# A spectral filter held in two buffers: its loads and stores cut in half by groups, and the second half moved behind the forward row moves

## The chip, the cores and the metric

The program runs on one core of one Trainium2 chip. The metric is the device time of one execution in microseconds (us), lower is better. Three runs of the kernel before took 339.59, 340.53 and 343.56 us, median 340.53. Five engines work side by side, each in its own program order: TensorE (PE, matmuls), VectorE (DVE), ScalarE (ACT), GpSimd (POOL) and SyncE (SP, which here does nothing but issue DMAs). An instruction of one engine waits for another's through semaphores.

## The reference

Forward, on x of 2048 x 448 in bf16, and then all gradients for a given output gradient:

```python
y  = irfft2(rfft2(layernorm(x)) * (w_r + 1j*w_i))      # over both axes; w_r, w_i: 2048 x 225
h  = x + y
u  = gelu(einsum("sd,sf->df", layernorm(layernorm(h)), w1) + b1)   # w1: 2048 x 1792
h2 = h + (einsum("df,fs->ds", u, w2) + b2).T                       # w2: 1792 x 2048
# results: h2 and the gradients of x, w_r, w_i, w1, b1, w2, b2
```

`w_r` and `w_i` are the filter. It is used twice: the forward transform is multiplied by it, and in the backward pass the gradient is multiplied by its conjugate, while the filter's own gradient (results `out_2` and `out_3`, of the same 2048 x 225 shape) is formed.

## The kernel before, in words

The order of PE, DVE, ACT and SP is that of the program text ("manual schedule"); only POOL's order is set by a planner. `clock`, `defer` and `fill` in the text serve that order: `fill(n)` puts n matmuls of an independent product between dependent ones, `defer` puts a DMA issue some matmuls later.

The stages around the change, in order:

- **Row stage** (loop over t in 0..15, lines 932 to 979). Tiles of x are normalised and folded on DVE, with the inverse standard deviations from Newton steps on POOL (`newton_gp`, lines 407 to 416). `row_a` and `row_b` (lines 661 and 671) turn them by two matmuls each. After every second `row_b` a **row move** (line 697) carries the result from SBUF to SBUF into `D2`; there are eight, seven issued by SP and the last by ACT. Between these stand matmuls of `dg` (line 845): 14 blocks of 16 matmuls of 128 x 448, which need block j of the transposed `w2`. Blocks 0 to 4 are turned on PE; **blocks 5 to 13 come by a DMA transpose each** (line 312), issued by SP into five slots. `cap` holds back blocks 9 to 13 until after the row loop (`held_w2`, lines 989 to 991).
- **Forward s2 stage** (`s2_stage`, line 704, called at line 999). Four sets s of four groups of 128 x 2 x 226. For each set PE does 48 small matmuls on `D2`, ACT copies the result to `Xs`, DVE multiplies by the filter (`w_mult`, line 753), and one turn later PE does 48 more on the product; the copies go by the **D3 moves** (line 740), four a set, into `D3`. The moves of the first three sets are issued by POOL, those of the last by SP, POOL and ACT. After that PE reads `D3` (`inv_rows`, line 765).
- **Backward**: the same s2 stage again (called at line 1384) with `bwd_mult` (line 1299), which also overwrites the filter by its gradient, set by set; then `inv_rows` with `gx_consumer` (line 1391), whose step t issues `GW_AT.count(t)` stores of that gradient. Between the small matmuls stand the weight gradients (`gw_gen`, line 1313), with their transposed inputs (`st_load`, `load_du`) and their stores, all on SP.

The filter lies in one buffer `rW` as (part c: real, imaginary) x (16 groups) x (225 columns) on 128 partitions; sets 0 and 1 use groups 0 to 7, sets 2 and 3 groups 8 to 15. Even partitions hold rows upward, odd partitions rows downward. `w_io` (line 580) is a generator of 18 DMAs, nine a part: four of 16 even partitions with 16 contiguous rows each (one run of 7200 bytes a partition), four of 16 odd partitions with rows in falling order (runs of 450 bytes), and one of 16 single rows. `W_AT` (line 924) says how many of the 18 loads are issued in which step t of the row loop; 14 go to SP, four to POOL (each behind a small clear on DVE, line 596, that keeps the planner from putting it earlier). All are issued by t = 6. The stores are the same 18 in the other direction, all on SP.

Of the kernel before, what the change touches and what calls it, by code (L numbers as in the profile page):

```python
# [124 lines left out]
def kernel(  # L125
# [123 lines left out]
    rW = region("rW", NG * 2 * KW)  # L249
# [326 lines left out]
    Wc = cut(rW, 0, 2, NG, DF)  # L576
    W = Wc.rearrange("p c g k -> p g c k")

    def w_io(dr, di, store):
        Wq = Wc.rearrange("(q s) c g k -> s q c g k", s=2)  # L580
        for c_, d in ((0, dr), (1, di)):
            moves = []
            for i in range(4):
                moves.append((Wq[0][16 * i:16 * i + 16, c_].rearrange("l g k -> l (g k)"), 16 * i, [[P * DF, 16], [1, 16 * DF]]))
                g0 = 0 if i else 1
                moves.append((Wq[1][16 * i:16 * i + 16, c_, g0:NG, :], P - 16 * i - g0,
                              [[P * DF, 16], [-DF, NG - g0], [1, DF]]))
            moves.append((Wq[1][0:16, c_, 0, :], 64, [[P * DF, 16], [1, DF]]))
            late = [m for n, m in enumerate(moves) if n in (0, 2, 4, 6)] if c_ and not store else []
            early = moves if not late else [m for n, m in enumerate(moves) if n not in (0, 2, 4, 6)]  # L590
            for n, (sb, row, dims) in enumerate(early + late):
                d_ap = bass.AP(d.tensor, d.offset + row * DF, dims)
                eng = nc.sync if n < len(early) else gp_
                if eng is gp_:
                    i = 32 * (n - len(early))
                    nc.vector.memset(Wc[i:i + 1, 1, 8, 0:1], 0.0)
                eng.dma_start(out=d_ap if store else sb, in_=sb if store else d_ap)
                yield
# [325 lines left out]
    W_AT = {**{t: 2 for t in range(6)}, 6: 6}  # L924
# [7 lines left out]
    for t in range(NT):  # L932
# [34 lines left out]
        if t in GROUPS:  # L967
            a, b = GROUPS[t]
            newton_gp(mvx[:, a:b, 1], rstd_x[:, a:b], slice(a, b))
        for _ in range(W_AT.get(t, 0)):  # L970
# [11 lines left out]
    for _ in w_loads:  # L982
        pass
# [4 lines left out]
    turn_biases, place_biases = load_biases()  # L988
    cap[0] = NFB
    while held_w2:  # L990
        held_w2.pop(0)()
    fill(4)
    gen_RT()
    fill(7)

    def fwd_mult(s, j, x, y):
        w_mult(x, set_of(W, s)[:, 2 * j:2 * j + 2], y, False)
# [485 lines left out]
```

## Time and profile before

| | |
|---|---|
| profiled execution, its own time | 340.34 us |
| its span, first to last instruction | 338.3 us |
| granted TensorE clock | 0.998 |
| PE busy | 330.2 us, 98% of the span |
| DVE, ACT, POOL busy | 251.7, 206.7, 84.6 us |
| DMA queue of SP and ACT's hardware path (q1) | 133288 packets, 73.13 MB, 84.5% of 16 engines' span |
| DMA queue of POOL (q0) | 2448 packets, 3.83 MB, 5.3% |
| runs | 339.59, 340.53, 343.56 us |

A busy PE is one on which some matmul is in flight, so 98% doesn't say that it is at its peak; the starts of its matmuls say where it stood. An SP row's time is the time of issuing, not of the transfer. "Idle before" stands in brackets behind the instruction that ended it, with what it waited for.

### The profile page before, as it was taken

How to read it: one execution, taken by the hardware profiler on the slowest of the kernel's cores; microseconds unless marked ns; L12 is line 12 of the kernel's file. 1: busy time of each engine (PE TensorE's matmuls, PEld its weight loads, DVE VectorE, ACT ScalarE, POOL GpSimd, SP SyncE). 2: the span in 40 equal slices, each digit the busy share in tenths (PEclk: the TensorE clock that was granted, in tenths of full speed). 3: DMA queues.
4: the chain of work that ended last, by engine and by line, in shares of the span. 5: the costliest groups of instructions: out<-in, count | busy, mean ns of one | idle time of the engine just before them, and what ended most of it. 6: DMA issues, size and time to landing. Idle time of an engine off the chain costs nothing.

```text
span 338.3 us, 7987 instructions
## 1 busy us (share of the span) xinstructions
PE 330.2 (98%) x2893; PEld 174.6 (52%) x2893; DVE 251.7 (74%) x670; ACT 206.7 (61%) x448; POOL 84.6 (25%) x254
## 2 busy tenths in 40 slices
PE   8999989999999999999999999999999999999995
PEld 4666554456545555555555555554344434555552
DVE  8998739827947888593227888786697993599994
ACT  6987666848965534423222346665588875588882
POOL 7767202412210000000001111210020222156670
PEclk9999999999999999999999999999999999999999
DMA  7999899959899999687877889837699999978885
GB/s 251 400 203 182 190 258 141 227 125 279 230 378 287 348 279 242 179 274 192 193 178 164 174 188 155 176 84 232 221 220 302 290 244 252 284 188 278 245 293 200
DMA packets 136198, 78.03 MB, mean 231 GB/s; under 512 B 86528, under 2 KB 127592, under 8 KB 136032
## 3 DMA queue, kind: packets, MB, share of 16 engines
q1 hardware_dynamic: 133288, 73.13, 84.5%
q0 software_dynamic: 2448, 3.83, 5.3%
q8 instruction: 22, 0.36, 0.5%
q10 hardware_dynamic: 424, 0.58, 0.5%
q14 instruction: 16, 0.13, 0.1%
HBM read 28.33 MB, written 22.04 MB: 149 GB/s over the span
## 4 chain that ended last, share of the span: by engine, by line
PE 83%; DVE 6%; DMA 4%; ACT 3%; issue 1%; POOL 1%; SPq 0%; DVEq 0%; ACTq 0%
PE ps_mm L220 68%; PE ps_ff L220 9%; PE ps_ff L225 3%; DMA r<-r 3%; ACT rO L84 2%; PE ps_mm L375 2%; DVE rS L84 2%; DVE r L84 1%; DMA r<-rX 1%; DVE rX L84 1%; DVE stats L84 1%; DVE rA L84 1%; ACT rE L84 1%; PE ps_mm L318 0%; DVE rG L84 0%
## 5 line engine op out<-in xcount | busy, mean ns | idle before, releaser
L220 PEld LDWEIGHTS <-r 128*128 128x128 bf16 (+2 forms) x628 | 58.6, 105 | 48.5 <-issue 3.0
L220 PEld LDWEIGHTS <-rS 128*128 128x128 bf16 (+1 forms) x468 | 36.2, 97 | 31.9 <-issue 6.0
L84 ACT CAST rO<-ps_mm 128x512 bf16<-128x512 f32 (+1 forms) x68 | 36.5, 584 | 14.5 <-PE ps_mm L220 11.9
L220 PE MATMUL ps_mm<-rD,r 128*128 128x448 bf16 x224 | 44.5, 352 | 0.0
L220 PEld LDWEIGHTS <-rst 128*128 128x128 bf16 (+1 forms) x320 | 23.9, 97 | 30.4 <-issue 12.1
L740 POOL DMA_DIRECT2D r<-r x29 | 17.4, 605 | 67.3 <-ACT r L84 56.7
L220 PE MATMUL ps_mm<-rC,rE 128*128 128x448 bf16 x144 | 32.1, 353 | 0.0
L220 PE MATMUL ps_mm<-rB,r 128*128 128x448 bf16 x160 | 31.2, 352 | 0.2 <-DVE rB L84 0.2
L220 PE MATMUL ps_mm<-rG,rst 128*128 128x512 bf16 (+1 forms) x128 | 28.5, 380 | 0.0
L220 PE MATMUL ps_mm<-r,rst 128*128 128x512 bf16 (+2 forms) x144 | 27.3, 345 | 0.0
L84 ACT ACTIVATE r<-ps_mm,rstd_h 128x448 bf16<-128x448 f32 x16 | 10.1, 634 | 26.8 <-PE ps_mm L220 26.8
L84 DVE SCALAR_TENSOR_TENSOR r<-ps_mm,b2col,r 128x448 bf16<-128x448 f32 x16 | 10.9, 682 | 19.9 <-PE ps_mm L220 18.6
L84 ACT ACTIVATE r<-rC 128x448 bf16<-128x448 bf16 x16 | 9.1, 570 | 26.7 <-DMA out_dram<-r 13.8
L84 ACT CAST r<-ps_ff 128x452 bf16<-128x452 f32 x43 | 23.1, 592 | 3.1 <-PE ps_ff L220 1.2
L1220 POOL TENSOR_SCALAR lcol<-lcol 128x1 f32<-128x1 f32 x16 | 8.5, 530 | 64.7 <-ACT r L84 64.7
L84 ACT ACTIVATE rG<-rG 128x896 bf16<-128x896 bf16 x14 | 13.3, 950 | 14.9 <-DVE rG L84 14.7
L220 PEld LDWEIGHTS <-rO 128*128 128x128 bf16 (+1 forms) x165 | 15.4, 98 | 12.3 <-ACT rO L84 0.2
L84 ACT CAST rS<-ps_ff 128x512 bf16<-128x512 f32 x31 | 18.0, 583 | 4.2 <-PE ps_ff L220 4.2
L220 PE MATMUL ps_ff<-csI,rAT 113*128 113x224 bf16 (+1 forms) x108 | 19.0, 298 | 0.2 <-DVE rA L84 0.2
L84 ACT CAST rG<-ps_mm 128x512 bf16<-128x512 f32 (+1 forms) x28 | 14.0, 539 | 7.6 <-PE ps_mm L220 7.5
L84 ACT CAST rAT<-ps_ff 113x512 bf16<-113x512 f32 x24 | 13.9, 586 | 7.7 <-PE ps_ff L220 7.5
L84 DVE TENSOR_SCALAR rG<-rG 128x896 bf16<-128x896 bf16 x28 | 10.9, 389 | 10.0 <-ACT rG L84 10.0
(200 smaller groups left out, 647.4 us busy)
## 6 DMA issues: line engine op xcount, KB each, us to landing
out_dram<-rO SPq DMA_DIRECT2D x34, 256.0 KB, 3.3
r<-in_B_w_dram SPq DMA_DIRECT2D x5, 1024.0 KB, 9.1
r<-r POOLq DMA_DIRECT2D x29, 113.0 KB, 5.5
out_dram<-rG SPq DMA_DIRECT2D x11, 256.0 KB, 3.1
r<-in_B_w_dram SPq DMA_DIRECT2D x3, 896.0 KB, 5.6
rS<-in_B_w_dram SPq DMA_DIRECT2D x3, 896.0 KB
rB<-in_B_w_dram SPq DMA_DIRECT2D x5, 512.0 KB, 8.1
r<-r SPq DMA_DIRECT2D x11, 226.0 KB, 2.5
```

Source lines behind the costliest of these rows:

```text
L84: fn(**kw)
L220: nc.tensor.matmul(out, lhsT=lhsT, rhs=rhs, start=start, stop=stop)
L225: nc.tensor.matmul(out, lhsT=lhsT, rhs=rhs, start=start, stop=stop)
L375: nc.tensor.matmul(idle[:, 0:D], lhsT=rAT[:, 0:P], rhs=rAT[:, 0:D], start=True, stop=True)
L740: defer(RESH_LAG, lambda g=g, ab=ab, eng=eng: eng.dma_start(out=D3[rowbase(g):rowbase(g) + 29:4, :, :, :], in_=ab), ab)
L1220: gp_.tensor_scalar(out=m1, in0=ms, scalar1=-1.0 / D, scalar2=None, op0=ALU.mult)
```

## The change: the filter in two buffers, and where its DMAs are issued

`rW` becomes two buffers `rW0` and `rW1` with eight groups each, for sets 0, 1 and for sets 2, 3. `w_io` goes through them one after the other. Every DMA of 16 partitions is cut in two by groups: runs of 3600 bytes on the even partitions, 7 or 8 runs of 450 bytes on the odd ones. There are now 34 DMAs each way: 18 for `rW0` (8 upward, then 8 downward and 2 of single rows) and 16 for `rW1` (8 downward, then 8 upward).

- **Loads of `rW0`** stay in the row loop by a new `W_AT`: 13 on SP up to t = 9, and 5 on POOL at t = 9, behind a clear on DVE of two columns of `rW0`. POOL's order now has all Newton steps of the row stage ahead of these five. The clear touches all partitions and stands behind the loads of the even ones, so the imaginary part of column 0 in groups 0 and 1 of the 64 even partitions (128 of 460,800 values) is left at zero.
- **Loads of `rW1`** come behind the row loop: 8 on POOL, behind a clear on DVE; 8 on SP, behind the seven row moves and the transpose of block 9, and ahead of the transposes of blocks 10 to 13. Before, the small loads of the biases stood between the row moves and block 9; now they stand behind block 10.
- `gen_RT` (one matmul and one copy, line 525) is called behind the forward s2 stage instead of ahead of it; its copy moves from DVE to ACT.
- **Stores**: 15 of the 34 are now issued in the backward s2 stage, five behind each of the sets' calls 2, 3 and 4; the other 19 in `gx_consumer`, by a `GW_AT` with 19 entries where there were 18.

SP issues one DMA fewer up to the last row move than before (13 filter loads instead of 14), 8 more between it and block 10, and 15 more in the backward s2 stage. The amount of data, and all work of PE, are the same.

```diff
@@ -246,7 +246,7 @@
     rS = region("rS", 7232)
     rO = region("rO", 3 * S)
     rX = region("rX", NG * 2 * KW)
-    rW = region("rW", NG * 2 * KW)
+    rW = [region(n, NG * DF) for n in ("rW0", "rW1")]
     r452 = region("r452", 8 * 452)
     rAT = region("rAT", 2 * 4 * P)
     rst = region("rst", 2 * 7 * P)
@@ -573,28 +573,28 @@
 
 
 
-    Wc = cut(rW, 0, 2, NG, DF)
-    W = Wc.rearrange("p c g k -> p g c k")
+    Wc = [cut(r, 0, 2, NG // 2, DF) for r in rW]
+
+    def w_set(s):
+        return Wc[s // 2].rearrange("p c (a b) k -> p b a c k", b=2)[:, s % 2]
 
     def w_io(dr, di, store):
-        Wq = Wc.rearrange("(q s) c g k -> s q c g k", s=2)
-        for c_, d in ((0, dr), (1, di)):
-            moves = []
-            for i in range(4):
-                moves.append((Wq[0][16 * i:16 * i + 16, c_].rearrange("l g k -> l (g k)"), 16 * i, [[P * DF, 16], [1, 16 * DF]]))
-                g0 = 0 if i else 1
-                moves.append((Wq[1][16 * i:16 * i + 16, c_, g0:NG, :], P - 16 * i - g0,
-                              [[P * DF, 16], [-DF, NG - g0], [1, DF]]))
-            moves.append((Wq[1][0:16, c_, 0, :], 64, [[P * DF, 16], [1, DF]]))
-            late = [m for n, m in enumerate(moves) if n in (0, 2, 4, 6)] if c_ and not store else []
-            early = moves if not late else [m for n, m in enumerate(moves) if n not in (0, 2, 4, 6)]
-            for n, (sb, row, dims) in enumerate(early + late):
+        H = NG // 2
+        for e in range(2):
+            Wq = Wc[e].rearrange("(q s) c g k -> s q c g k", s=2)
+            ups, dns = [], []
+            for c_, d in ((0, dr), (1, di)):
+                for i in range(4):
+                    b, g0 = slice(16 * i, 16 * i + 16), 0 if e or i else 1
+                    ups.append((d, Wq[0][b, c_].rearrange("l g k -> l (g k)"), 16 * i + H * e, [[P * DF, 16], [1, H * DF]]))
+                    dns.append((d, Wq[1][b, c_, g0:H], P - 16 * i - H * e - g0, [[P * DF, 16], [-DF, H - g0], [1, DF]]))
+                if not e:
+                    dns.append((d, Wq[1][0:16, c_, 0], 64, [[P * DF, 16], [1, DF]]))
+            moves = dns + ups if e else ups + dns
+            for n, (d, sb, row, dims) in enumerate(moves):
+                on_gp = not store and (n < 8 if e else n >= 13)
                 d_ap = bass.AP(d.tensor, d.offset + row * DF, dims)
-                eng = nc.sync if n < len(early) else gp_
-                if eng is gp_:
-                    i = 32 * (n - len(early))
-                    nc.vector.memset(Wc[i:i + 1, 1, 8, 0:1], 0.0)
-                eng.dma_start(out=d_ap if store else sb, in_=sb if store else d_ap)
+                (gp_ if on_gp else nc.sync).dma_start(out=d_ap if store else sb, in_=sb if store else d_ap)
                 yield
 
     r452_ring = ring(r452, 0, 8, 2, KW)
@@ -921,7 +921,7 @@
     GROUPS = {0: (6, 8), 1: (8, 10), 3: (10, 12), 5: (12, 14), 7: (14, 16)}
     STATS = {0: (6, 7), 1: (8, 9), **{t: (t + 8,) for t in range(2, 8)}}
     INV_S = {11: 0, 12: 1, 13: 2, 14: 3}
-    W_AT = {**{t: 2 for t in range(6)}, 6: 6}
+    W_AT = {0: 2, 1: 1, 2: 2, 3: 1, 4: 2, **{t: 1 for t in range(5, 9)}, 9: 6}
     FILL_A = (4, 4, 8, 12, 6, 3, 3, 4, 5, 3, 3, 2, 2, 2, 3, 3)
     FILL_B = (0, 0, 2, 2, 2, 2, 4, 4, 3, 2, 2, 2, 2, 2, 2, 2)
     def uv_step():
@@ -967,6 +967,8 @@
         if t in GROUPS:
             a, b = GROUPS[t]
             newton_gp(mvx[:, a:b, 1], rstd_x[:, a:b], slice(a, b))
+        if t == 9:
+            nc.vector.memset(Wc[0][:, 1, 0:2, 0:1], 0.0)
         for _ in range(W_AT.get(t, 0)):
             next(w_loads, None)
         if t in INV_S:
@@ -979,25 +981,29 @@
         fill(FILL_B[t])
     for _ in uv:
         pass
-    for _ in w_loads:
-        pass
+    nc.vector.memset(Wc[1][:, :, 0, 0:1], 0.0)
+    for _ in range(8):
+        next(w_loads)
     gp_.memset(csF[:, 0, :, 0:1], 1.0)
     gen_inv_d(0)
     fill(6)
     gen_inv_d(1)
-    turn_biases, place_biases = load_biases()
     cap[0] = NFB
+    held_w2.pop(0)()
+    for _ in w_loads:
+        pass
     while held_w2:
         held_w2.pop(0)()
+    turn_biases, place_biases = load_biases()
     fill(4)
-    gen_RT()
     fill(7)
 
     def fwd_mult(s, j, x, y):
-        w_mult(x, set_of(W, s)[:, 2 * j:2 * j + 2], y, False)
+        w_mult(x, w_set(s)[:, 2 * j:2 * j + 2], y, False)
 
     s2_stage(lambda s: set_of(Xs, s), fwd_mult, 8, (8,) * 5, 0, split=True)
     sc.activation(out=warm, in_=eps_h, func=ACT.Sqrt)
+    gen_RT()
     fill(21)
 
     w1c_ring = Ring([cut(r, o, NT, 256) for r, o in ((r2, 0), (r2, NT * 256), (rO, S))])
@@ -1298,7 +1304,7 @@
 
     def bwd_mult(s, j, xc, y):
         xs = set_of(Xs, s)[:, 2 * j:2 * j + 2, :, 0:DF]
-        gw = set_of(W, s)[:, 2 * j:2 * j + 2]
+        gw = w_set(s)[:, 2 * j:2 * j + 2]
         w_mult(xc, gw, y, True)
         xc = xc[:, :, :, 0:DF]
         p1, p2 = (p_ring.next()[:, :, :, 0:DF] for _ in range(2))
@@ -1381,12 +1387,18 @@
         rows(t)
     fill(N_FILL_B[2])
     Meter.slack = 7.0
-    s2_stage(lambda s: X_ring.next(), bwd_mult, 14, (14, 28, 14, 28, 20), N_FILL_B[4], {0: lambda: load_du(1), 1: lambda: (load_du(0), load_xall(0)), 2: lambda: load_xall(1), 3: lambda: load_du(2)},
+    g_out = w_io(out_2, out_3, True)
+
+    def store_gw(n):
+        for _ in range(n):
+            next(g_out)
+
+    s2_stage(lambda s: X_ring.next(), bwd_mult, 14, (14, 28, 14, 28, 20), N_FILL_B[4], {0: lambda: load_du(1), 1: lambda: (load_du(0), load_xall(0)), 2: lambda: (load_xall(1), store_gw(5)),
+              3: lambda: (load_du(2), store_gw(5)), 4: lambda: store_gw(5)},
              2.0 * INV_SD)
     Meter.slack = 2.0
-    g_out = w_io(out_2, out_3, True)
     X_AT = {0: 2, 4: 3}
-    GW_AT = tuple(range(12)) + tuple(range(1, 12, 2))
+    GW_AT = tuple(range(12)) + (1, 3, 5, 7, 9, 10, 11)
 
     def gx_consumer(t, py):
         if t in X_AT:
```

## The prediction

> **What bounds the kernel now.** I read the page's busy times, then PE's waits, then the timelines of PE, POOL and SP around each of them.
>
> ```profile
> PE 330.2 (98%) x2893; PEld 174.6 (52%) x2893; DVE 251.7 (74%) x670; ACT 206.7 (61%) x448; POOL 84.6 (25%) x254
> ```
> ```profile
> PE ps_mm L375 <- DVE rS L628: 1.2, 1, 1.2
> PE ps_ff L225 <- DMA r<-rX: 0.9, 1, 0.9
> PE ps_ff L220 <- DMA r<-r: 0.7, 2, 0.5
> PE ps_ff L220 <- DVE rS L84: 0.7, 1, 0.7
> PE ps_ff L225 <- DVE rS L84: 0.3, 1, 0.3
> ```
>
> The waits (total us, times, longest) come to 4.2 us with the two of 0.2 that follow them. Elsewhere matmuls follow each other: 495 in the 94.03 us from 94.13 of the chain, 190 ns each. The change leaves PE's work alone, so the most it can win is the waits it reaches: 0.7 (row stage), 0.9 (last row move), 0.7 (D3, forward and backward), about 2.3 us. What it can lose has no such end. Where the three stand:
>
> ```profile
> 35.02 0.40 PE L220 MATMUL ps_ff<-rX,rS 128*128 128x128 bf16 x4 [0.66 <-DVE rS L84]
> ...
> 48.40 0.62 PE L225 MATMUL ps_ff<-r,Vt 32*32 32x452 bf16 x12 [0.91 <-DMA r<-rX]
> ...
> 75.37 0.85 PE L220 MATMUL ps_ff<-RTm,r 128*113 128x128 bf16 x12 [0.49 <-DMA r<-r]
> ```
>
> (The backward one is 0.24 us at 288.93.) POOL's and SP's timelines say why the first two are late:
>
> ```profile
> 28.34 0.20 POOL L413 TENSOR_TENSOR nt_f<-rstd_x 128x2 f32<-128x2 f32 x1
> 28.57 1.76 POOL L597 DMA_DIRECT2D rW<-in_A_w_i_dram  x3
> 30.34 0.24 POOL L414 TENSOR_TENSOR nt_f<-nt_f,mvx 128x2 f32<-128x2 f32 x1
> ```
> ```profile
> 30.71 1.28 SPq L597 DMA_DIRECT2D rW<-in_A_w_i_dram  x2
> 32.09 5.12 SPq L312 DMA_TRANSPOSE rE<-in_B_w_dram  x1
> 37.26 1.24 SPq L597 DMA_DIRECT2D rW<-in_A_w_i_dram  x2
> 38.60 0.59 SPq L697 DMA_DIRECT2D r<-r  x1
> 39.29 2.78 SPq L312 DMA_TRANSPOSE rO<-in_B_w_dram  x1
> 42.17 1.23 SPq L697 DMA_DIRECT2D r<-r  x2
> 43.50 1.85 SPq L697 DMA_DIRECT2D r<-rX  x3
> 45.45 0.79 SPq L824 DMA_DIRECT2D rst<-in_grad_out_dram  x1
> ...
> 47.67 1.90 SPq L312 DMA_TRANSPOSE rO<-in_B_w_dram  x1
> 49.66 9.97 SPq L312 DMA_TRANSPOSE rE<-in_B_w_dram  x3
> 59.73 5.26 SPq L312 DMA_TRANSPOSE rO<-in_B_w_dram  x1
> ```
>
> POOL issues four filter loads in the middle of a Newton group. On SP, issuing a transpose takes 1.6 to 5.3 us, for the DMA engines are full (share 1.10, 1.15, 0.94 in the stretches of 8 us from 20 to 44); six row moves pile up behind and leave between 42.17 and 44.81, the last ACT's, landing 3.7 us after its issue at 44.30.
>
> **Row stage: what is removed.** POOL's four issues cost the Newton group 1.76 + 0.53 us; DVE then waited for POOL 0.81 us (33.38) and 0.78 us (36.20), and PE 0.66. The five new POOL loads stand behind all Newton steps: **-0.66 us**. What is late next is DVE's folding, with no slack that the trace shows; the gain lies between 0 and 0.66. The new clear on DVE at t = 9 (59 ns a clear now) waits for four upward loads; they are issued behind block 6's transpose (26.7 us now) and land 4.1 to 11.2 us after issue, the median 5.8, so at about 33 us. The clear's place is near 34. Were it late, row matrices and evictions behind it would wait for it, 1 to 2 us at the far end; by the median, nothing.
>
> Half the filter's transfer leaves this stage. In the trace's packet records 4,096 packets of 450 bytes (loads and stores) took 38 ns each and 256 of 7200 bytes 491 ns; over 16 engines that is 8.8 us a direction. So 4.4 us of DMA time leave a stage of 32 us that has none free. The transposes should issue faster, and the row moves leave as their data come; only the last must then land behind the last copy. Its 3.7 us should fall to the 2.9 or 3.0 of the others: **-0.8 us** of the wait of 0.91, with 0 as the other end. POOL's eight `rW1` loads start as this move is under way. D3 moves from POOL took 3.8 to 6.9 us to land, so their first packets come late for it; if not, up to 0.9 us is given back.
>
> **Behind the row moves: what is added.** The s2 stage now starts some 1.5 us earlier, and everything after it is due 1.5 us earlier. SP's chain: block 9 goes out at about 44.7 (row moves end 0.66 earlier, biases gone) instead of 47.67. Eight `rW1` loads at 0.63 (issue and gap, three took 1.89) take 5.0 us, so block 10 goes out at 51.7 instead of 49.66, **+2.0**; the biases (45.45 to 47.58) follow, so blocks 11 to 13 go out **+4.1**. Queued behind them on SP are the D3 moves of set 3; SP stood idle from 64.99 to 69.86, so 4.1 fits under 4.9, or 3.4 once these are due earlier, overshooting by 0.7 at worst. By DMA time the second half adds 4.4 us to a stretch whose share is 0.99, 1.14, 1.20 from 44 to 68: the same delay.
>
> When are the blocks due? The packets (2,048 of 256 bytes a block) of blocks 10, 11, 12, 13 ended at 55.0, 59.3, 61.1, 66.3. By PE's timeline their matmuls begin at 59.7, 64.4, 68.3, 72.06, all 1.5 earlier after. With the delays: 57.0 against 58.2; 63.4 against 62.9; 65.2 against 66.8; 70.4 against 70.6. Block 11 is short by 0.5, block 13 comes just in time. I take **+0.6 us** here; ends: 0, if faster transposes pay it back, and 3.3 us, if all four are 3 us later still. `rW1` itself is due when set 2 is multiplied, near 59; it is issued by 52 and landing takes up to 11.2 us: 63, so at worst 4 us late, by the median (58) just not. The D3 wait of 0.49 stays: it is the moves' own transit of 4.6 us. `gen_RT`'s copy moves behind ACT's table load at 71.49 (1.28 us), ready near 73.4, due 75.37: nothing; its matmul is the same.
>
> **Backward.** Fifteen stores at 0.62 (median) add 9.3 us to SP between 261 and 285, where its rows leave some 10 us idle, and 15/34 of 8.8 = 3.9 us of DMA time to a stretch at a share of 1.0. Behind the first five stand a transpose and two stores (1.4 us late); the slot of the store that landed at 270.1 is needed at 273.1. Behind the second five stand the transposes for `gw_gen`, about 3 us late: the one that landed at 278.5 is needed near 284. Hidden. What isn't is the end of the stage: the last five stores come at 281 to 284, with the D3 moves of set 3 (4.1 to 5.8 us to land, PE waiting 0.24). Five stores are 1.5 us of DMA time, so 0 to +1.5.
>
> Here one page matters. The profile has D3 on its own queue, q0, and SP's stores on q1; in the packet records both move packets in every microsecond from 282 to 288. The Trainium skill, "DMA: Bandwidth & Descriptors", section "Queues, rings and completion order", says that each DMA engine goes round-robin between the queues that have work. By that rule, and the trace agrees, stores lengthen q1's line and leave D3's half of the engines: the cost would be near 0.
>
> I take **+0.3**, nearer to 0 since q1 already had work all the time. After 289 the stage has 19 stores instead of 18, half as long: nothing, PE has no wait there.
>
> The loads go from 112.5 to 56.25 KB each. The records have the same 38 ns for a run of 450 bytes whether 256 or 240 of them make a DMA. A run of 3600 bytes isn't in them: by bytes 245 ns, at worst the 491 of the long one. That worst case adds 3.9 us of DMA time each way, half of it behind the row moves, about 2 us more on blocks 11 and 13; I take the 245. The same page of the Trainium skill has a rule against the change ("Bandwidth", "Measured"): transfers under 64 KB are dominated by their descriptors. By it the sum would be some 2 us higher; no run shows it yet.
>
> **Sum:** 340.34 - 0.66 - 0.8 + 0.6 + 0.3 = 339.8 us, against a median of 340.53 whose runs span 4 us. Unchanged, in short; 1% (3.4 us) is about what a measurement can tell.
>
> **Rivals.** (1) **Blocks 10 to 13 turn into PE's wait**: 340.34 - 1.46 + 3.3 + 0.3 = 342.5, and 344.5 with 2 us for slow short runs. Place: PE's `dg` matmuls from 57 to 72. It decides once block 13's packets end later than 70.6, that is, 4.3 us later than now. For it: the line of SP's transposes and the full engines; against it: 3 us of early start and 8 us in SP's slow issues that may shorten. 0.15 slower by over 1%, 0.12 below that. (2) **The filter is hidden anyway**: the row moves still leave late, as the transposes need SP by themselves; 0 gain, 340.6 with the +0.3. 0.20. (3) **Everything wins**: no cost, D3's waits gone too: 340.34 - 2.3 = 338; with the small stalls between row matmuls 337. 0.15, over 1% only 0.05. Forecast (339 to 340.3): 0.38.
>
> Leaving out 1 in 10 on each side, the range is 337.3 to 343.2. Faster by over 1% 0.05, slower by over 1% 0.15, the same 0.80.
>
> **What would show it.** No POOL issue among the Newton steps, and PE's wait of 0.66 gone; row moves on SP from 25 to 44 instead of in a heap; no wait for `r<-rX` at the start of s2, near 46.9; waits of PE for `rE` or `rO` transposes, if any, at 62 and 70; DVE never waiting for `rW1`; PE's wait for D3 near 287 under 1 us. I am wrong if `dg` matmuls wait for 2 us or more, if DVE stands at the clear, or if the row moves still go in a heap.

## The result and the profile after

The changed kernel is slower, by less than one per cent. Its median is 344.28 us (20 runs, 341.56 to 347.68) against 341.00 us of the kernel before (20 runs beside them, 338.90 to 344.43); the ratio is 1.0077, with a 95% interval of 1.0048 to 1.0106, that is 2.6 us on 340.34. The profiled execution took 345.56 us with a span of 343.8, against 340.34 and 338.3, so it lies 1.3 us above its own median: its rows say where the time goes, and the ratio how much it is. The ratios leave disturbed executions out; those profiled of three cut kernels (no loads, twice, and all loads on POOL) were such, so their places in the table below are read for the order of what happens, not for a time.

Where the two profiled executions stand, in us from the span's start:

| | before | after | difference | gained or lost since |
|---|---|---|---|---|
| s2 stage begins | 48.40 | 46.76 | -1.64 | -1.64 |
| forward D3 read | 75.37 | 79.32 | +3.95 | +5.59 |
| backward D3 read | 288.93 | 293.28 | +4.35 | +0.40 |
| last matmul ends | 334.65 | 339.45 | +4.80 | +0.45 |
| span | 338.3 | 343.8 | +5.5 | +0.7 |

The row stage won about what was forecast, and the s2 stage lost over three times as much. PE's busy time and PE's waits (us in total, times, longest) in the changed kernel:

```profile
PE 330.8 (96%) x2893; PEld 174.6 (51%) x2893; DVE 250.5 (73%) x667; ACT 206.6 (60%) x449; POOL 88.9 (26%) x263
```
```profile
PE ps_mm L220 <- DMA rE<-in_B_w_dram: 2.6, 3, 1.1
PE ps_mm L220 <- DMA rO<-in_B_w_dram: 1.7, 1, 1.7
PE ps_ff L225 <- issue: 1.3, 1, 1.3
PE ps_mm L375 <- DVE rS L628: 1.2, 1, 1.2
PE ps_ff L220 <- issue: 0.6, 1, 0.6
PE ps_mm L220 <- DVE rG L84: 0.3, 1, 0.3
PE ps_ff L220 <- DMA r<-r: 0.3, 1, 0.3
```

The waits for `r<-rX` (0.9) and for DVE's `rS` (0.7) are gone; 4.3 us for the transposed blocks in `rE` and `rO` have come, which the kernel before did not have at all. PE's timeline shows one at each block, 10 to 13, and no wait at the head of the stage:

```profile
46.76 0.40 PE L225 MATMUL ps_ff<-r,Vt 32*32 32x452 bf16 x12
...
54.49 0.51 PE L225 MATMUL ps_ff<-rS,UVT 32*32 32x452 bf16 x32 [1.26 <-issue]
...
59.52 0.36 PE L220 MATMUL ps_mm<-rC,rE 128*128 128x448 bf16 x1 [0.51 <-DMA rE<-in_B_w_dram]
...
65.37 0.36 PE L220 MATMUL ps_mm<-rC,rE 128*128 128x448 bf16 x1 [1.02 <-DMA rE<-in_B_w_dram]
...
70.48 0.36 PE L220 MATMUL ps_mm<-rC,rE 128*128 128x448 bf16 x1 [1.09 <-DMA rE<-in_B_w_dram]
...
76.21 2.82 PE L220 MATMUL ps_mm<-rC,rO 128*128 128x448 bf16 x14 [1.67 <-DMA rO<-in_B_w_dram]
79.32 0.85 PE L220 MATMUL ps_ff<-RTm,r 128*113 128x128 bf16 x12 [0.29 <-DMA r<-r]
```

SP's own timeline (start, duration of the issue) says what stands ahead of these blocks:

```profile
35.85 0.58 SPq L697 DMA_DIRECT2D r<-r  x1
37.82 5.86 SPq L697 DMA_DIRECT2D r<-rX  x3
43.77 2.22 SPq L312 DMA_TRANSPOSE rO<-in_B_w_dram  x1
46.08 2.48 SPq L597 DMA_DIRECT2D rW<-in_A_w_r_dram  x4
48.60 4.73 SPq L597 DMA_DIRECT2D rW<-in_A_w_i_dram  x4
53.53 2.46 SPq L312 DMA_TRANSPOSE rE<-in_B_w_dram  x1
...
57.58 7.40 SPq L312 DMA_TRANSPOSE rE<-in_B_w_dram  x2
65.10 4.69 SPq L312 DMA_TRANSPOSE rO<-in_B_w_dram  x1
```

The row moves leave as their data come. Block 9 goes out 3.9 us earlier than before, and block 10 3.9 us later: the eight loads took 7.45 us, not 5.0, since the last of them stood until 52.83, when block 9, eight DMAs earlier on SP, had landed (SP's DMAs signal through eight semaphores in turn). Block 13 is 5.4 us later.

How late the blocks are on the other end is in the DMA view, whose last number is us from issue to landing. Block 13 alone, from 58 to 72 us in the kernel before and from 62 to 78 us in the changed one:

```profile
rO<-in_B_w_dram SPq DMA_TRANSPOSE x1, 10.6
```
```profile
rO<-in_B_w_dram SPq DMA_TRANSPOSE x1, 11.1
```

Issued at 59.73 and 65.10, they land at 70.32 and 76.16. The first of these two rows was there to be read before the prediction, which went by the end of block 13's packets, 66.3, instead.

### The profile page after: what moved, and what is told of

It is laid out like the page before. It is cut to its first block, busy times and chain, and to the rows that moved or that the text cites. A ratio compares the mean times of both kernels' runs of the same rounds, so it can differ in the third digit from the quotient of the medians.

```text
span 343.8 us, 8033 instructions
## 1 busy us (share of the span) xinstructions
PE 330.8 (96%) x2893; PEld 174.6 (51%) x2893; DVE 250.5 (73%) x667; ACT 206.6 (60%) x449; POOL 88.9 (26%) x263
## 4 chain that ended last, share of the span: by engine, by line
PE 78%; DMA 7%; DVE 7%; ACT 4%; issue 2%; DVEq 0%; POOL 0%; ACTq 0%
PE ps_mm L220 65%; PE ps_ff L220 8%; DVE r L84 4%; DMA rE<-in_B_w_dram 3%; DMA rO<-in_B_w_dram 3%; PE ps_ff L225 2%; PE ps_mm L375 2%; ACT rO L84 2%; DVE rS L84 1%; DVE rA L84 1%; DMA out_dram<-r 1%; ACT rE L84 1%; DVE stats L84 0%; ACT rG L84 0%; ACT rAT L84 0%
## 5 line engine op out<-in xcount | busy, mean ns | idle before, releaser
L220 PE MATMUL ps_mm<-rC,rO 128*128 128x448 bf16 x80 | 18.1, 353 | 1.7 <-DMA rO<-in_B_w_dram 1.7
L220 PEld LDWEIGHTS <-rE 128*128 128x128 bf16 x144 | 12.7, 98 | 13.0 <-DMA rE<-in_B_w_dram 3.9
```

Source lines behind the costliest of these rows:

```text
L220: nc.tensor.matmul(out, lhsT=lhsT, rhs=rhs, start=start, stop=stop)
```

## The experiments

Ratios are to the kernel before, from runs on the same chip. "Blocks" is PE's wait for `rE` and `rO` from 44 us to D3; the places are those of the profiled execution.

| kernel | ratio, 95% interval | s2 begins | D3 read | blocks |
|---|---|---|---|---|
| before | 1 | 48.40 | 75.37 | 0 |
| changed | 1.0077 (1.0048 to 1.0106) | 46.76 | 79.32 | 4.3 |
| no loads of the second half | 1.0018 (0.9980 to 1.0055) | 48.63 | 79.46 | 0 |
| the same, cleared later | 1.0033 (0.9994 to 1.0072) | 50.03 | 82.32 | 0 |
| POOL's eight loads alone | 1.0190 (1.0126 to 1.0254) | 48.28 | 83.51 | 1.4 |
| SP's eight loads alone | 1.0237 (1.0175 to 1.0298) | 49.05 | 85.66 | 7.8 |
| all sixteen, an eighth of the bytes | 1.0196 (1.0147 to 1.0245) | 48.28 | 82.18 | 4.5 |
| the same, cleared later | 1.0203 (1.0140 to 1.0266) | 49.32 | 80.26 | 2.8 |
| all sixteen on POOL | 1.0119 (1.0048 to 1.0191) | 46.06 | 82.71 | 0.4 |
| blocks 9 and 10 ahead of SP's loads | 1.0212 (1.0169 to 1.0255) | 45.66 | 81.61 | 3.6 |
| before, eight tiny loads more on SP | 1.0146 (1.0089 to 1.0203) | 47.09 | 83.39 | 3.8 |
| before, eight loads more on POOL | 1.0092 (1.0055 to 1.0128) | 49.51 | 77.53 | 0 |
| all loads in the row loop, unheld | 1.0293 (1.0243 to 1.0343) | 57.77 | 85.55 | 0 |
| all loads in the row loop | none (median 346.34 to 340.97) | 50.24 | 79.75 | 0 |
| second half from 36 to 44 us | 1.0103 (1.0063 to 1.0143) | 49.08 | 77.65 | 0 |
| block 9 in the row loop | 1.0067 (1.0027 to 1.0107) | 46.93 | 76.24 | 0 |
| before, POOL's loads late | 1.0031 (0.9999 to 1.0063) | 47.97 | 76.38 | 0 |
| before, POOL's loads on SP | 1.0081 (1.0050 to 1.0112) | 48.37 | 75.12 | 0 |
| stores behind D3 | 1.0214 (1.0163 to 1.0266) | 46.94 | 78.33 | 4.0 |
| fifteen stores left out | 1.0071 (1.0034 to 1.0109) | 46.20 | 78.62 | 3.9 |

### What the sixteen loads cost

```diff
-    nc.vector.memset(Wc[1][:, :, 0, 0:1], 0.0)
-    for _ in range(8):
-        next(w_loads)
...
     held_w2.pop(0)()
-    for _ in w_loads:
-        pass
...
+        if t == 10:
+            gp_.memset(Wc[1].rearrange("p c g k -> p (c g k)"), 0.0)
```

> The changed kernel without the 16 loads of the second half of the filter: that half is set to zero by POOL at row step 10 instead, so the products of sets 2 and 3 are zero. It prices the second half's forward transfer by itself. Theory: without it blocks 9 to 13 go out on SP one behind the other, PE waits under 0.5 us in all for rE and rO, the s2 stage starts near 46.8 and D3 is read near 74; ratio 0.993 to 0.997. Rival, that the transposes are late by themselves once the s2 stage starts earlier (the full engines): PE still waits 2 us or more for rE and rO, ratio 0.999 or more.

No wait for a block is left, as every theory of the loads had it. The ratio is 0.0059 below that of the changed kernel, 2.0 us, although the clearing of the missing half ran ahead on POOL and PE waited 1.1 us for DVE's `rX` at 8 us, where the changed kernel has no wait. A second such kernel holds the clearing back with one DVE clear at the same row step:

> The changed kernel without the 16 loads of the second half, once more: the earlier such kernel's clearing of that half ran ahead to POOL's first instructions and cost PE 1.3 us near 7 us; here POOL clears it behind its Newton steps. The second half is zero, so the products of sets 2 and 3 are zero. First corner of four (no POOL loads, no SP loads). Any theory of the loads: no wait for rE or rO over 0.5 us, s2 starts at 46.2 to 47.2, forward D3 read at 73.5 to 75, ratio 0.993 to 0.998. If PE still waits 2 us or more for the transposes, the loads are not the cause.

Again no wait for a block, and again a cost of its own: PE waited 2.3 us for DVE's `rX` near 40 us, behind the clearing. Neither came under the kernel before, as the theory had it (0.993 to 0.997 and 0.993 to 0.998). In part that can be those 1.1 and 2.3 us: if nothing hid them, the sixteen loads cost 3.1 us and 3.8 us by the two kernels; without them 2.0 and 1.5 us. In both profiled executions PE also waited 2.8 and 3.0 us for "issue" in the s2 stage, of which more below. The first difference from the changed kernel (0.0059) is just clear of the two intervals, the second (0.0044) is not. So the loads make the waits for the blocks, and most likely the larger part of the loss; its size stays open.

### SP's line or the transfer

Two kernels were to tell these apart. One puts all sixteen loads on POOL:

```diff
-                on_gp = not store and (n < 8 if e else n >= 13)
+                on_gp = not store and (e or n >= 13)
...
```

> The changed kernel with all 16 loads of the second half on POOL, none on SP: the same bytes in the same stretch, but nothing in front of SP's transposes. Theory that SP's line makes the loss (8 issues, one of them waiting for block 9 to land): block 10 goes out near 48 instead of 53.5, the waits for rE and rO fall under 1 us, ratio 0.995 to 1.000. Rival, that the 5 us of DMA time make it wherever they are issued: blocks 10 to 13 end as late as now, PE waits 3 us or more for them, ratio 1.004 to 1.008. A third outcome: POOL's last loads are issued near 54 and land after 59, when DVE multiplies set 2, and DVE waits for them.

Block 10 was indeed issued at 45.23, but this one issue now took 6.89 us, and blocks 11 to 13 went out at 54.61, 59.90 and 64.26, only 3.0, 1.9 and 0.8 us earlier than with SP's eight loads in front; block 13 landed at 77.40, even later than there (76.16). The third outcome came too: DVE waited 6.5 and 1.3 us for `rW` at set 2. PE waited only 0.4 us for blocks, but 2.0 us for DVE and 3.0 us for "issue" ahead of its last blocks, which made them due later; so this kernel doesn't tell the two theories apart. The other kernel keeps all sixteen instructions and cuts each to one group of eight (the same clearing as above):

```diff
+                if e and not store:
+                    if len(dims) == 2:
+                        sb, dims = sb[:, 0:DF], [dims[0], [1, DF]]
+                    else:
+                        sb, dims = sb[:, 0], [dims[0], dims[2]]
```

> The changed kernel with each of the 16 loads of the second half cut to one group of eight (450 bytes a partition instead of 3600): the same instructions on SP and POOL in the same places, one eighth of the bytes. The other seven groups of that half are zero, set by POOL at row step 10, so most of the products of sets 2 and 3 are zero. Theory that DMA time makes the loss: blocks 10 to 13 land 4 us or more earlier than in the changed kernel, PE waits under 1 us in all for rE and rO, and the ratio is that of the kernel without these loads, 1.000 to 1.004. Rival, that SP's line of eight issues and its wait for the DMA eight before make it: block 10 still goes out near 53, PE waits 3 us or more, ratio 1.005 to 1.009.

SP's line is as long as before: block 10 was issued at 54.05 and block 11 at 58.17, as in the changed kernel (53.53 and 57.58), though an eighth of the bytes moved: this speaks for SP's line. PE stood 4.46 us at block 11. The windows (after the span: busy us of PE, PEld, DVE, ACT, POOL, then the granted clock, the DMA share and GB/s) show engines that were half idle while SP issued, and what the long wait did to the clock:

```profile
52.00:60.00 8.00, 7.79 (x202) 3.90 (x201) 7.46 (x17) 6.13 (x14) 2.42 (x4) 1.00 0.54 103
60.00:68.00 8.00, 4.15 (x105) 2.00 (x78) 6.61 (x15) 4.44 (x10) 2.36 (x4) 0.98 1.07 161
68.00:76.00 8.00, 7.39 (x113) 3.23 (x113) 0.00 (x0) 2.38 (x5) 2.36 (x4) 0.60 1.27 170
```

The corners were then run on one chip with the later clearing: no loads (above), POOL's eight alone, SP's eight alone, and all sixteen tiny.

```diff
 POOL's eight alone:
     held_w2.pop(0)()
-    for _ in w_loads:
-        pass
 SP's eight alone:
+                if e and n < 8 and not store:
+                    continue
...
-    for _ in range(8):
-        next(w_loads)
```

> The same with POOL's eight loads of the second half back (half of its bytes, 2.5 us of DMA time) and SP's eight left out, so that the even partitions of that half are zero. Theory SP's line: as without any load, ratio 0.993 to 0.999, waits for rE and rO under 0.5 us. Theory DMA time: half of the loss, waits of 1.5 to 2.5 us, ratio 1.000 to 1.004.

> The same with SP's eight loads and without POOL's eight, so that the odd partitions of the second half are zero. Theory SP's line: block 10 goes out 4 us late or more, near 53, waits for rE and rO of 3 us or more, the ratio of the changed kernel, 1.005 to 1.009. Theory DMA time: as with POOL's eight alone, waits of 1.5 to 2.5 us, ratio 1.000 to 1.004.

> The changed kernel with its 16 loads of the second half at one eighth of their bytes (one group of eight; the other seven are zero), as once before, but with the clearing behind POOL's Newton steps. Theory SP's line: blocks 10 to 13 as late as in the changed kernel or later, ratio 1.005 or more, and over 1.010 if one single wait reaches 2.6 us, since the granted clock then stands near half for some 3 us behind it. Theory DMA time: no wait over 0.5 us, ratio 0.994 to 1.000.

For either half alone both theories were too small; the sixteen tiny ones came as the theory of SP's line had it, with a single wait of 2.83 us and a ratio over 1.010. With no loads the ratio is 1.0033; with SP's eight it is 1.0237, with POOL's eight 1.0190, and with sixteen tiny ones 1.0203. Either half alone costs more than 1.5%, so the two are not terms of a sum. All four kernels carry the clearing, and both halves at full size were not run with it; the changed kernel, which has both and no clearing, is at 1.0077, below either half alone. So the clearing takes part in these losses, and they are no price of the loads by themselves. In the kernel with POOL's eight, block 10's issue on SP took 6.59 us, and PE waited for blocks (1.4), for DVE (1.8), for D3 (2.5) and for "issue" (3.1). In the kernel with sixteen tiny ones nearly nothing moved from 52 to 58 us while SP issued; block 10 left at 56.95.

The order on SP was also turned round, with blocks 9 and 10 both ahead of its loads:

```diff
     held_w2.pop(0)()
+    if held_w2:
+        held_w2.pop(0)()
     for _ in w_loads:
```

> The changed kernel with SP's transposes of blocks 9 and 10 both ahead of its eight loads of the second half. Theory that SP's order makes the lateness: block 10 goes out near 46.5 instead of 53.5, PE's waits for blocks 9 and 10 go (1.3 and 0.5 us), those for 11 to 13 stay near 1 us each or shrink by 1 us together; the loads land some 4 us later, near 61, and DVE then waits for them at set 2 (58.5) by up to 2.5 us; ratio 1.002 to 1.008. Rival, DMA time alone: the ends of blocks 11 to 13 stay within 0.5 us of 63, 68 and 72.6, and the ratio stays at 1.006 to 1.009.

Block 10 did go out early, at 44.91, but its issue took 6.84 us beside POOL's loads; SP's loads landed past 61, and DVE stood 4.3 and 3.2 us at set 2, longer than expected. Blocks 11 to 13 went out at 60.67, 63.91 and 68.39, later than in the changed kernel. Neither of these two orders has room on SP for both.

### One cost at a time, added to the kernel before

All these carried other edits. The last two add one cost each to the kernel before and take nothing away: eight loads into a free part of `rB` behind block 9's transpose, once tiny on SP, once 56.25 KB each on POOL.

```diff
+    pad = cut(rB, 0, n)
+    nc.vector.memset(pad[:, 0:1], 0.0)
...
+    held_w2.pop(0)()
+    for i in range(8):
+        eng.dma_start(out=pad[16 * i:16 * i + 16],
+                      in_=bass.AP(A_w_r.tensor, A_w_r.offset + 16 * i * DF, [[P * DF, 16], [1, n]]))
     while held_w2:
         held_w2.pop(0)()
 tiny on SP:   n = 225,  eng = nc.sync
 on POOL:      n = 1800, eng = gp_
```

> The kernel before with nothing taken away and one cost added: eight tiny loads (450 bytes a partition, 58 KB in all, into a free buffer that nobody reads) on SP between block 9's transpose and block 10's. No other edit, and no clearing that costs PE anything. SP's line alone: eight issues of 0.63 us put block 10 off by 5 us or more (49.66 before), block 13 lands 4 us or more later than 70.3, past its due time of 72.06; PE waits 2 to 4 us for rE and rO, ratio 1.006 to 1.015. Theory DMA time: 58 KB are nothing, blocks land within 1 us of before, ratio 0.998 to 1.003.

> The kernel before with the other cost added alone: eight loads of 56.25 KB on POOL (16 partitions of 3600 bytes, into a free buffer that nobody reads), issued behind the row moves, while blocks 9 and 10 are transposed; SP's program is untouched. DMA theory, with transposes that slow down beside other transfers: block 9's and 10's transposes take 2 us or more longer to issue and land, block 13 lands 2 us or more later, PE waits 1 to 4 us for rE and rO, ratio 1.004 to 1.015. Theory SP's line: SP issues what it issued before, blocks land within 1 us of before, ratio 0.998 to 1.003.

SP's line is enough by itself. SP's timeline and PE's waits from 44 to 86 us of the kernel with eight tiny loads:

```profile
46.03 2.15 SPq L312 DMA_TRANSPOSE rO<-in_B_w_dram  x1
48.27 4.38 SPq L994 DMA_DIRECT2D rB<-in_A_w_r_dram  x8
52.75 9.93 SPq L312 DMA_TRANSPOSE rE<-in_B_w_dram  x3
62.81 9.10 SPq L312 DMA_TRANSPOSE rO<-in_B_w_dram  x1
```
```profile
PE ps_mm L220 <- DMA rO<-in_B_w_dram: 2.8, 1, 2.8
PE ps_ff L225 <- issue: 2.2, 1, 2.2
PE ps_mm L220 <- DMA rE<-in_B_w_dram: 1.0, 1, 1.0
```

Block 10 is 3.1 us later than in the kernel before, not 5 as expected; block 13 is issued 3.1 us later (62.81 for 59.73) and lands 8.9 us later, at 79.17. So 58 KB and 4.4 us of SP cost 1.46%, and a delay grows on its way: the late transposes fall among POOL's D3 moves. (The profiled execution, 348.27, is the slowest of the six, whose median is 345.50; its "issue" wait of 2.2 us is part of that.) The packet records show where. In the kernel before, block 13's packets run alone from 65 us, over 1,100 a microsecond of 18 ns each; in this one the packets of blocks 12 and 13 go at 1 to 580 a microsecond from 66 to 73 us, from 68 to 70 beside D3's 4520-byte packets.

The bytes on POOL hit something else: blocks 10 to 13 go out 0.9 to 2.0 us later than before (block 13 lands at 71.91, 1.6 us later) and PE has no wait for them, against the theory of the DMA time, whose ratio came true all the same. But PE waited 2.1 us for the last row move, which those loads met on its way, and the clock fell behind that wait. The first wait of this kernel:

```profile
PE ps_ff L225 <- DMA r<-rX: 2.1, 1, 2.1
```

So both costs are real and each hits the work next to it: SP's line the transposes, the bytes whatever is in flight.

### Is there a better place

In the row loop, as in the kernel before but in halves (SP's 21 loads in steps 0 to 6, POOL's 13 at step 9):

```diff
-    W_AT = {0: 2, 1: 1, 2: 2, 3: 1, 4: 2, **{t: 1 for t in range(5, 9)}, 9: 6}
+    W_AT = {**{t: 3 for t in range(7)}, 9: 13}
```

> The changed kernel, but with nothing left behind the row moves: the 21 half-sized loads of SP go out three a row step in steps 0 to 6, the 13 of POOL behind its Newton steps at step 9. Two buffers, halved DMAs, POOL's relief and the stores stay as changed. Theory that moving the second half behind the row moves makes the loss: the waits for blocks 10 to 13 go (under 0.5 us in all), the row stage is full again and its last row move late, the s2 stage starts at 47.5 to 48.4, and the ratio is 0.997 to 1.002. Rival, that halved DMAs with shorter rows cost the DMA engines more wherever they stand: the ratio stays at 1.005 or more, with the row moves later than in the kernel before.

This did not test what it was meant to: without the clear that holds them, POOL's eight loads of the second half were placed ahead of everything on POOL, DVE waited 2.78 us for `x` at 11 us, and PE stood 5.5 us. With clears at steps 4 and 9, in one kernel for all steps and in one for the stretch from 36 to 44 us, where the changed kernel's DMA share is only 0.58:

```diff
+        for c in range(2):
+            if t == W1_HOLD[c]:
+                nc.vector.memset(Wc[1][:, c, 0, 0:1], 0.0)
+        for _ in range(W1_AT.get(t, 0)):
+            next(w1_loads, None)
 all steps:      W1_HOLD, W1_AT = (4, 9), {4: 2, 5: 2, 6: 2, 7: 2, 9: 8}
 36 to 44 us:    W1_HOLD, W1_AT = (9, 9), {9: 8, 10: 2, 11: 2, 12: 2, 13: 2}
```

> The test that the run with all loads in the row loop could not make, since eight loads on POOL ran ahead to the front of the program there: here DVE's clears hold them. The changed kernel with nothing left behind the row moves: SP's 21 half-sized loads in row steps 0 to 7, POOL's 13 at step 9 behind its Newton steps. Theory that moving the second half behind the row moves makes the loss: PE's waits for rE and rO under 0.5 us in all, the s2 stage starts at 47 to 48.4, D3 read at 74 to 75.5, ratio 0.996 to 1.001. Rival, that half-sized loads cost SP and the DMA engines more wherever they stand: row moves later than in the kernel before, s2 start after 48.4, ratio 1.004 or more.

> The changed kernel with the second half's loads in the stretch from 36 to 44 us, where its DMA engines were busy at only 0.58: POOL's eight (the imaginary plane) behind its Newton steps at row step 9, SP's eight (the real plane) two a step in steps 10 to 13, between the row moves. Theory that the loss is only the place of these loads: blocks 9 to 13 go out on SP as early as in the kernel before or earlier, PE waits under 0.5 us for rE and rO, the s2 stage starts at 46.8 to 47.6, D3 read near 74; ratio 0.993 to 0.998. Rival: SP's row moves are late behind the loads, s2 starts at 48 or later, and the time is that of the kernel before, 0.998 to 1.003.

Neither waits for a block, as the theory of the place said, and both begin the s2 stage later than the kernel before, as the rivals said: PE waits 3.3 and 2.9 us for the last row move, `r<-rX`. The first has no ratio: its six runs spread from 340.57 to 347.81. The loss has moved, not gone. What did help is to fill that stretch with the transpose that is late afterwards:

```diff
-CAP = 9
+CAP = 10
...
-    held_w2.pop(0)()
     for _ in w_loads:
```

> The changed kernel with block 9's transpose issued inside the row loop as soon as its buffer is free (nine blocks were the limit there, now ten), ahead of the last four row moves, and SP's eight loads of the second half first behind them. It puts 3.7 us of DMA time into the stretch from 36 to 44 us where the engines were busy at 0.58, so that everything queued behind is earlier. Theory that the loss is DMA time in the wrong stretch: blocks 10 to 13 land 2 to 4 us earlier, PE's waits for rE and rO fall from 4.3 to under 1.5 us, ratio 0.998 to 1.003. Rival: the transpose takes SP and the engines from the last row moves, PE waits 2 to 3 us for r<-rX at the start of s2 as in the kernels with loads in the row loop, ratio 1.005 to 1.010.

PE's waits from 44 to 86 us of this kernel:

```profile
PE ps_ff L225 <- issue: 2.0, 1, 2.0
PE ps_ff L220 <- DMA r<-r: 1.0, 1, 1.0
PE ps_ff L225 <- DVE rS L84: 0.2, 1, 0.2
```

The early start of s2 is kept, all 4.3 us of waits for blocks are gone, and D3 is read 3.1 us earlier than in the changed kernel. The ratio, though, is 1.0067: not to be told from the changed kernel's, above what the theory expected and where the rival had it, but without the rival's wait for `r<-rX`; no version here beats the kernel before. The profiled execution (342.38, against 340.34 of the kernel before) shows most of that loss: D3 is read 0.9 us later though s2 began 1.5 us earlier, with the "issue" wait of 2.0 us and D3's of 1.0 between, and behind the backward D3 another 1.3 us go. So a kernel without any wait for a block loses as much by its ratio as the changed one. In the changed kernel's profiled execution the waits for the blocks are the largest loss; that they are the whole of the ratio's is not shown. The "issue" wait varies from 0 to 3.0 us over the profiled executions here.

### The Newton steps without POOL's loads

```diff
 before, late:   W_AT = {**{t: 2 for t in range(7)}, 9: 4}
 before, on SP:  eng = nc.sync
```

> The kernel before, one buffer and whole-sized loads, with nothing changed but the place of POOL's four loads: behind its Newton steps, at row step 9. It measures my term of 0.66 us by itself. Theory: PE's wait of 0.66 us on DVE in the row stage goes, the s2 stage starts up to 0.7 us earlier, ratio 0.997 to 0.999 or not to be told from 1. Rival: the loads land too late for set 0 or delay the last row move, and the start of s2 stays at 48.4; ratio 1.000 to 1.003.

> The kernel before with POOL's four whole-sized loads put on SP in the same row steps, so that POOL has no load at all and its Newton steps run through. My term of 0.66 us without any load behind them: PE's wait of 0.66 us at 35 goes, and the s2 stage starts 0.3 to 0.7 us earlier if SP's four more issues (0.62 us each) are covered; ratio 0.997 to 1.000. Rival: SP's line delays the row moves and transposes by 2.5 us, the start of s2 is later than 48.4, ratio 1.002 to 1.008.

Alone the term of 0.66 us is worth nothing measurable. With the loads late, PE's wait in the row stage goes and PE reaches s2 at 45.9, where it waits 2.1 us for the last row move that these loads now meet: s2 begins 0.43 us earlier and D3 is read 1.0 us later. With the loads on SP PE's wait in the row stage falls to 0.32 us, but PE waits 0.97 us at the head of s2, which begins at 48.37 as before. Why the latter is slower by 0.8% stays open: its profiled execution, 341.34, is the fastest of its twelve and reads D3 0.25 us earlier than the kernel before.

### The stores

```diff
 stores behind D3:  no store_gw in s2_stage; GW_AT has all 34
 left out:          the first 15 stores are not issued
```

> The changed kernel with all its stores of the filter gradient back behind the backward D3 (34 half-sized stores in the GX steps), the forward part as changed. Forward theory: blocks 10 to 13 make the whole loss, so PE again reads the forward D3 near 79 us, the gap there and in the four dg waits stays at 4 to 5 us, and the ratio to before is 1.005 to 1.008. Store theory: a third of the loss or more comes from the 15 stores put into the backward s2 stage; then the ratio falls to 1.003 or below, and the backward D3 is read 0.4 us earlier relative to the forward one. If the GX steps cannot take 34 stores, their ring waits grow and the ratio rises over 1.008.

> The changed kernel without the 15 stores of the filter gradient in the backward s2 stage: they are left out, so those parts of two outputs are never written; the 19 stores behind it stay. It prices my backward term of 0.3 us. By the term: 0 to 0.5 us less than the changed kernel, ratio 1.006 to 1.008, and PE's wait for the backward D3 (0.79 us) back near 0.24. Rival, that these stores cost a third of the loss or more: ratio 1.003 to 1.005, the backward D3 earlier by 1 us or more relative to the forward one.

Leaving the fifteen stores out changes the ratio by 0.0006, inside its interval: 0.2 us, give or take 1.6, and the backward D3 is no earlier. My 0.3 us is not contradicted, but this is too coarse to confirm it. Putting them all behind D3 costs 0.0137 more, 4.7 us: DVE's waits behind 290 us are

```profile
DVE r L84 <- DMA out_dram<-r: 5.1, 2, 3.6
```

against none in the kernel before and 1.4 us in the changed one, and PE waits 4.0 us for DVE at the end. Thirty-four half-sized stores are too many for SP beside the GX rows; nineteen are nearly too many.

## Why the prediction was wrong

The forecast was 339.8 us and "the same", with a range of 337.3 to 343.2. The median is 344.28 us and the ratio puts the kernel at 343.0; a loss had been given 0.27 of the chance.

**The step that failed is the date of the blocks.** The term of +0.6 us compared the end of each block's 256-byte packets with the time its matmuls were due. What releases PE is the landing, and the rows have it later: in the kernel before, block 10's packets end at 55.0 and it lands at 55.66, but block 13's end at 66.3 and it lands at 70.32, behind the D3 moves that POOL had issued meanwhile. Its margin before was therefore 72.06 less 70.32, 1.74 us, not the 5.8 that the packets show; against the earlier due time of 70.6 it was 0.3 us, not the 4.3 that I gave as the point from which the rival decides. With that one number put right the prediction's own sum gives a loss: 70.32 + 4.1 = 74.4, due at 70.6, so PE waits 3.8 us, and 340.34 - 1.46 + 3.8 + 0.3 = 343.0. That it meets the ratio's time so well is luck, since the delay was larger too: block 13 landed at 76.16, 5.6 us after it was due, which is what the profiled execution lost there (4.3 us for the blocks and 1.3 us for "issue"), and the sum would be 344.8. Rival (1) was this mechanism, in its place, priced at 342.5 and given 0.27.

The delay itself was taken too small: +2.0 at block 10 and +4.1 at blocks 11 to 13, where the issues have +3.9, +4.1, +6.3 and +5.4, and block 13's landing +5.8. Two parts of it were wrong. SP's eight loads took 7.45 us instead of 5.0, for the eighth waited for block 9. And I counted SP's line and the DMA time as one delay seen from two sides; the runs show two costs, either of which is enough.

The other steps:

- **Row stage, -0.66 and -0.8:** s2 begins 1.64 us earlier in the changed kernel, against 1.46. The sum is right partly by luck. The first term alone gains nothing (1.0031) while a row move is what ends last. The second was read from the wrong move: PE did not wait for ACT's, which carries the groups of sets 2 and 3, but for SP's last one, issued at 44.81 before. ACT's move did not fall from 3.7 us to 2.9; it took 6.0 us beside POOL's loads (rows below), and landed at 49.70, 2.9 us after s2 had begun. What gained was that SP's last move was issued at 43.15 and landed at 45.84.
- **The clear on DVE:** it stands at 34.10, 0.06 us long, and waits for nothing. Right.
- **`rW1` in time for set 2:** DVE never waits for it in the changed kernel. Right, but only just: with SP's loads behind block 10 it waited.
- **3600-byte runs at 245 ns:** the 256 of the second half took 316 ns on average from 44 to 80 us, 5.1 us of all 16 engines instead of 4.4. The Trainium skill, "DMA: Bandwidth & Descriptors", sections "Bandwidth" and "Measured", has the rule that transfers under 64 KB are dominated by descriptors. No run here tests it: that an eighth of the bytes was no faster (1.0203) fits the rule, but fits SP's line as well.
- **Backward +0.3:** +0.40 between the two D3 reads, and 0.2, give or take 1.6, by the kernel without the stores. Not contradicted. The wait there is named "issue" (0.6), not D3.
- **After 289, nothing:** wrong by 1.15 us in the profiled execution (0.45 to the last matmul, 0.7 behind it). DVE waits 1.4 us for the stores of GX, which stand on SP behind twenty-four filter stores: nineteen planned there and five more that left the s2 stage late.
- **Not foreseen at all:** the "issue" waits, 1.3 us at 53 us and 0.6 at 293.

ACT's row move, the last number again us from issue to landing, in the kernel before and in the changed one:

```profile
r<-rX ACTq DMA_DIRECT2D x1, 226.0 KB, 3.7
```
```profile
r<-rX ACTq DMA_DIRECT2D x1, 226.0 KB, 6.0
```

How much of the ratio's 2.6 us each of these has is not settled: the profiled executions differ by 5.2 us, and the kernel without any wait for blocks is as slow by its ratio as the one with 4.3 us of them.

## What to carry to other kernels

Date a transfer by the row that says when it landed, not by its packets: the margin here was 1.7 us and looked like 5.8. Before a load is moved "behind" a stage, write down what else is queued on that issuing engine up to the next wait, with landings, and what the same DMA engines carry then; eight tiny loads in a queue that feeds the bound engine cost 1.46% here. And a free stretch is better given to the transfer that will be late next than to the one that happens to be moved: here that took away every wait for a block, though not the loss.

## What the runs showed of the hardware

**A transpose can land long after its own packets.** In four cases where SP's transpose ran beside POOL's D3 moves, its landing followed the last of those that POOL had issued before by 0.1 to 0.4 us, however long its own packets had ended: 69.92 and then 70.32 (packets to 66.3) before, 70.22 and 70.43 (block 12), 75.92 and 76.16 (block 13) in the changed kernel, 71.78 and 71.91 (packets to 67.9) with eight loads more on POOL. It is no fixed rule: block 11 of the changed kernel released PE at 65.37, 0.15 us ahead of the landing (65.52) of a move that POOL had issued 0.35 us before SP was done with the transpose. With none beside it, block 10 of the kernel before landed 0.7 us after its packets. The Trainium skill, "DMA: Bandwidth & Descriptors", section "Queues, rings and completion order", says that the semaphore's increment is a strongly ordered write, which lands only after every earlier write of that DMA engine, across its queues. The four cases agree with it.

**Transposes are slower beside other transfers.** At its fastest a block alone moves over 1,100 packets a microsecond at 18 ns each. Beside loads or D3 moves there were mostly 100 to 600 a microsecond at 20 to 90 ns. How much of that is sharing is not settled: in the kernel before, 61 and 249 a microsecond (at 52 and 56 us) went at 222 and 201 ns with nothing beside them but an instruction packet. In that kernel D3's packets start at 61.1 and at 66.32, where the packets of blocks 12 and 13 end (61.1 and 66.34).

**PE's "issue" waits end behind an instruction packet.** In the packet records, each such wait of over 0.5 us in the forward s2 stage ends 1.2 to 1.9 us after the end of a 16,384-byte packet on the queue that the profile calls instruction: 52.9 and 54.49 in the changed kernel, 65.1 and 66.48 with eight tiny loads, 64.2 and 65.40 with block 9 in the row loop. That the packet is what PE waits for is argued from this order, not shown: the kernel before has such packets (at 62.4 and 68.2 us) and no such wait.

**An idle of 2 us can halve the clock.** In the clock records of all runs, an idle of PE goes with a granted clock of 0.50 for 3.41 us, or for twice that, or with none. Idles of 1.90, 2.08 and 2.11 us (blocks 9 and 10 ahead; eight loads more on POOL; POOL's loads late) had such a dip; idles of 1.99 to 2.36 us in six other kernels had none; every idle of 2.8 us or more up to D3 had one. Sixteen `dg` matmuls that took 3.2 us at the full clock took 5.34 us in the kernel with sixteen tiny loads. The Trainium skill, "TensorE: Matmul & The Clock Gate", section "Part 1: The HAM clock gate (the "warmup" mystery)", has the clock halved after an idle window of about 3.4 us that runs freely. The length of the dips agrees with that window; as a limit for the idle it does not hold here, since shorter idles were enough at times. The changed kernel, whose four waits for blocks are 0.5 to 1.7 us long, has no dip up to its last matmul, so such dips are one cost that only the kernels with a longer single wait have.
